# The first pair of heads loaded, cast and transposed head by head; batch 0's masks all on TensorE; PSUM banks from one list

## The chip, the cores and the metric

The kernel runs on one core of one Trainium2 chip. A core has TensorE (PE in the profile; PEld is its weight loads), VectorE (DVE), ScalarE (ACT), GpSimd (POOL) and SyncE (SP), which run side by side and wait for each other by semaphores. SP, ACT and POOL also issue the DMA transfers between DRAM and the on-chip memory SBUF. TensorE writes its results to PSUM, eight banks of 512 fp32 columns by 128 partitions. The metric is the device time of one execution in microseconds (us), lower is better.

## The reference

Attention over 4 batches, 8 heads, 768 positions and head size 64, followed by a two-layer feed-forward block with a PReLU. Heads 0, 2 and 6 ("retrieval") see all earlier positions; the other five ("streaming") see the first 4 positions and the last 64.

```
scores = scale * q @ k.T                      # per batch and head, 768 x 768
scores = where(mask, scores, -1e9)            # causal, or sink + window
a = softmax(scores);  x = a @ v               # 4 * 768 tokens of 8 * 64
h = x @ w_in                                  # 512 -> 2048
g = max(h, 0) + alpha * min(h, 0)
out = g @ w_out                               # 2048 -> 512
```

## The kernel before, in words

Heads are worked in pairs: pair n = 0 to 15, batch n // 4, heads PAIRS[n % 4] = (0,1), (2,3), (6,7), (4,5). Two heads of 64 fill the 128 partitions. A pair goes through these steps, and the document names them as the changed kernel does.

- Load: q, k and v by DMA into fp32 buffers (load_q L124, load_k L130, load_v L142), four buffers each. SP issues them, except pair 0's first k head and alpha, which ACT issues.
- Cast to bf16 (whole_q L179, whole_k L188, whole_v L208). In batch 0, pair 0's q is cast by VectorE for both heads at once (L183), its k by ScalarE for the first head and by VectorE for the second (L196); pairs 1 to 3 and all v of batch 0 are cast by GpSimd.
- Transpose: for pairs 0 to 7, six TensorE transposes each for q and k against an identity matrix (Tn, L291) into a PSUM bank, both heads at once. Tq (L298) is then copied to qT by ScalarE (L301), Tk (L303) to kT by VectorE (L314, L320 to L322), one head at a time; kT holds zeros in the other head's 64 partitions, so that a score matmul runs over 128 partitions. From pair 8 on, DMA transposes take their place.
- Scores S.n.head.part (S_retr L345, S_stream L378): matmuls of kT and qT into PSUM (L362, L393; L412 from pair 8), then the exponential by ScalarE into eR or eS (L370, L400, L415). In batch 0 a part uses two banks at once. The mask is either a further matmul of the identity with a tile of 0 and -30000, added into the same bank before the exponential (L365, L396), or a product with a 0/1 tile by VectorE after it (L375, L404, L420). In batch 0 TensorE adds all masks but those of pair 3's first head.
- A.n.head (AV, L452): 13 or 27 matmuls of eS or eR with v, whose column 64 of ones gives the softmax's sum; VectorE takes the reciprocal (L472) and multiplies (L473) into xn.
- X.n (L476): seven transposes of xn on TensorE and a copy to xT by VectorE (L487); for most pairs from 8 on, a DMA transpose.

A batch's 768 tokens then go through the feed-forward block as two token tiles, 512 and 256 wide, t = 0 to 7. P.t.f (P1, L505) is one bank of the first layer: four matmuls, one for each pair's 128 rows of xT (L516), ScalarE's ReLU of the negative (neg, L523) and VectorE's product and sum into g (L526). O.t.s.u (P2, L531) is a quarter of the second layer's 16 matmuls for 128 tokens (L536); after the fourth, ScalarE copies to ot (L541) and a DMA writes it out (L544).

The order of the work is that of the instructions as the Python code emits them; each engine runs its own in that order. First come the fills, the making of the masks, 36 matmuls of the identity with itself (L592 to L594) and pair 0's casts and transposes. A loop (L631) then lays out batch 0's pairs. Token tile 0's first blocks begin with the first three of their four matmuls (LEAD = 4 blocks, L657 to L667), with X3 between the second and the third block; then come the last columns and the other blocks. From pair 4 on, the attention of a batch is interleaved with the feed-forward work of the batch before by a budget (L712 to L731).

PSUM banks have fixed roles (L76): sc0 and sc1 for scores, m0 and m1 in turn for A, X and transposes, mm0, mm1, mm2 and m2 for the feed-forward block. ff_bank (L498) gives that block the bank which an assumed clock says is free first; before pair 4 and after pair 15 it may use the score banks too.

Of the kernel before, what the change touches and what calls it, by code (L numbers as in the profile page):

```python
# [10 lines left out]
DT = mybir.dt  # L11


@with_exitstack
def kernel(
# [60 lines left out]
    BANK = {"sc0": 0, "sc1": 1, "mm2": 2, "m2": 3, "mm0": 4, "mm1": 5, "m0": 6, "m1": 7}  # L76

    def bank(tag):
        return P[:, BANK[tag], :]

    def bank_bf(tag):
        return P[:, BANK[tag], :].bitcast(bf16)

# [80 lines left out]
    def load(n):  # L164
        load_q(n)
        load_k(n)
        load_v(n)

    natq, natk = {}, {}
# [7 lines left out]


    def whole_q(n):  # L179
        nat = natq[n] = NAT0[0][n] if n < 4 else NATQ[n % 2]  # L180
        copy = nc.gpsimd.tensor_copy if 0 < n < 6 else nc.scalar.copy if 0 < n < CROSS else nc.vector.tensor_copy
        flat = qf[n % NF].rearrange("p a b d -> p (a b d)")[:, 0:12 * D]
        copy(nat.rearrange("p i (h d) -> p h i d", h=2), flat.rearrange("p (h i d) -> p h i d", h=2, d=D))  # L183
        if n >= CROSS:
            nc.sync.dma_start(qT[n % NK][:, 0:S].rearrange("p (i r) -> p i r", r=128),
                              nat.rearrange("p i c -> p (i c)"), transpose=True)

    def whole_k(n):  # L188
        if n < CROSS:
            natk[n] = NAT0[1][n] if n < 4 else NATK1[n % 2]  # L190
            for hh, h in enumerate(heads(n)):
                copy = nc.gpsimd.tensor_copy if 0 < n < 6 else nc.scalar.copy if n == hh == 0 else nc.vector.tensor_copy

                T = row_tokens(n, h)
                flat = kf[n % NF].rearrange("p a b d -> p (a b d)")[:, 6 * D * hh:6 * D * (hh + 1)]
                copy(natk[n][:, :, D * hh:D * (hh + 1)].rearrange("p (t i) d -> p t i d", t=T),  # L196
                     flat.rearrange("p (i t d) -> p t i d", t=T, d=D))
            return
        flat = NATK[n % 2]
        rows = flat.rearrange("p (h x) -> p h x", h=2)[:, :, 0:896].rearrange("p h (t c) -> p h t c", c=128)  # L200
        nc.vector.tensor_copy(rows[:, :, :, 0:D], kf[n % NF].rearrange("p t h d -> p h t d"))
        sinks(n, rows)
        for hh, h in enumerate(heads(n)):
            nt = 6 if RETR[h] else 7
            nc.sync.dma_start(kTs[n % NK][hh][:, 0:128 * nt].rearrange("p (i r) -> p i r", r=128),
                              flat[:, 896 * hh:896 * hh + 128 * nt], transpose=True)

    def whole_v(n):  # L208
        vv = vb[n % NV]
        (nc.gpsimd if n < 6 else nc.vector).tensor_copy(vv[:, :, :, 0:D], vf[n % NF])  # L210
        sinks(n, vv.rearrange("p t h c -> p h t c"))

    for i in range(NF):
        nc.vector.memset(vf[i][:, 6, :, :], 0.0)
    load_q(0)
    load_k(0)
    alpha_r = wpool.tile([16, 128], fp32, name="alpha_r")
    nc.scalar.dma_start(alpha_r, moe_alpha.rearrange("(a p) -> a p", p=128))
    for n in range(1, 4):
        load_q(n)  # L220
        load_k(n)
        load_v(n - 1)
    load_v(3)

    zero = const.tile([128, 1], bf16, name="zero")
    nc.vector.memset(zero, 0.0)
    one = const.tile([128, 1], bf16, name="one")
    nc.vector.memset(one, 1.0)
    ident = const.tile([128, 128], bf16, name="ident")
    make_identity(nc, ident)  # L230
    ident_f = const.tile([16, 16], fp32, name="ident_f")
# [111 lines left out]
    def S_retr(n, hh, m):  # L343
        if m == 0:
            take_e(n, hh)  # L345
# [423 lines left out]
```

The softmax here doesn't subtract the row's maximum and nothing guards it: scores larger than these inputs give would overflow.

## Time and profile before

| | |
|---|---|
| median of 6 runs (range) | 242.29 us (241.66 to 242.57) |
| the profiled execution's own time | 242.38 us |
| its span, first to last instruction | 240.6 us |
| PE busy | 227.0 us (94%) |
| DVE busy | 165.3 us (69%) |
| ACT busy | 144.0 us (60%) |
| POOL busy | 43.8 us (18%) |
| granted TensorE clock, mean | 0.999 |

The page's busy times are of one profiled execution, on an axis that starts near its first instruction. A matmul's time includes its way through the array, so neighbouring matmuls overlap: "0.86 PE P L516 x4" in the chain is four matmuls one behind the other, 0.216 us each, though one alone shows 0.38 us. An engine's line with a bracket tells how long it stood idle before, and what came last of what it waited for. The chain of the page is followed back from the last instruction; it names the work that set the end. A few per cent of the matmul records can be missing.

By stages the profile falls into: fills and loads (0 to 5.7 us), batch 0's attention (5.7 to 28.4), the first feed-forward tile alone (28.4 to 43), attention of batches 1 to 3 with feed-forward work between (43 to 195), and the feed-forward rest (195 to 240.6).

### The profile page before, as it was taken

The page shows a single profiled execution, that of the slowest core. Times are in us where ns is not written, and L with a number is a line of the kernel's source. Part 1 is how long each engine was busy: PE and PEld are TensorE (multiplying, and loading weights), DVE is VectorE, ACT ScalarE, POOL GpSimd, SP SyncE. Part 2 cuts the span into 40 slices and gives each one's busy share as a digit, 9 for nine tenths or more (in the row PEclk, how much of TensorE's full clock was granted, in tenths as well). Part 3 has the DMA queues.
Part 4 walks back from the last instruction along what each step waited for, and adds up shares of the span by engine and source line. Part 5 has one row for each costly group of instructions (what it writes and reads, how often), then busy time and mean ns, then how long its engine had stood idle before and what let it go on. Part 6 is the DMA issues. An engine that isn't in the chain of part 4 may idle for free.

```text
span 240.6 us, 5234 instructions
## 1 busy us (share of the span) xinstructions
PE 227.0 (94%) x1987; PEld 143.5 (60%) x2017; DVE 165.3 (69%) x405; ACT 144.0 (60%) x265; POOL 43.8 (18%) x90
## 2 busy tenths in 40 slices
PE   6799899989987999999999999999999999999994
PEld 6688645557655755455666655556666544465553
DVE  7697878868798867989577858884665465633410
ACT  5888277847855757776655557866554354523220
POOL 5668960632010100000000000000000000000000
PEclk9999999999999999999999999999999999999999
DMA  6999999999999999999999992603131101011112
GB/s 207 294 239 171 226 204 197 246 279 248 253 213 131 245 191 226 211 167 216 199 224 203 225 175 66 120 3 77 46 78 44 46 0 45 0 61 73 44 44 90
DMA packets 90513, 36.25 MB, mean 151 GB/s; under 512 B 77672, under 2 KB 88696, under 8 KB 90488
## 3 DMA queue, kind: packets, MB, share of 16 engines
q1 hardware_dynamic: 84504, 26.66, 58.0%
q0 software_dynamic: 5664, 8.91, 16.5%
q10 hardware_dynamic: 320, 0.34, 0.5%
q8 instruction: 16, 0.26, 0.4%
q14 instruction: 9, 0.07, 0.1%
HBM read 27.55 MB, written 6.29 MB: 141 GB/s over the span
## 4 chain that ended last, share of the span: by engine, by line
PE 83%; DVE 7%; ACT 6%; issue 2%; ACTq 0%; DVEq 0%
PE P L516 34%; PE P L536 31%; PE P L467 6%; PE P L362 5%; ACT eR L370 2%; PE P L412 2%; PE P L291 2%; ACT eS L400 2%; PE P L553 1%; DVE xn L473 1%; PE P L486 1%; DVE g L526 1%; DVE eS L404 1%; PE P L393 1%; ACT neg L523 1%
## 5 line engine op out<-in xcount | busy, mean ns | idle before, releaser
L526 DVE SCALAR_TENSOR_TENSOR g<-neg,oma,P 128x512 bf16<-128x512 f32 (+1 forms) x128 | 74.7, 612 | 44.5 <-ACT neg L523 42.8
L516 PE MATMUL P<-xT,w_in_b 128*128 128x512 bf16 (+1 forms) x505 | 94.5, 325 | 0.4
L536 PE MATMUL P<-w_out_b,g 128*128 128x512 bf16 x345 | 88.7, 379 | 1.2
L523 ACT ACTIVATE neg<-P 128x512 f32<-128x512 f32 x96 | 57.2, 598 | 51.2 <-PE P L516 47.6
L516 PEld LDWEIGHTS <-w_in_b 128*128 128x128 bf16 x512 | 48.0, 98 | 29.3 <-issue 0.5
L536 PEld LDWEIGHTS <-g 128*128 128x128 bf16 x368 | 33.9, 98 | 30.1
L370 ACT ACTIVATE eR<-P 128x488 bf16<-128x488 f32 (+4 forms) x63 | 38.4, 620 | 13.7 <-PE P L362 11.8
L544 POOL DMA_DIRECT2D out_dram<-ot x18 | 9.8, 546 | 134.0 <-ACT ot L541 134.0
L362 PE MATMUL P<-qT,kT 128*128 128x488 bf16 (+17 forms) x132 | 24.7, 273 | 1.5 <-ACT eS L400 0.6
L473 DVE TENSOR_TENSOR xn<-P,rcp 128x448 bf16<-128x448 f32 x32 | 20.0, 624 | 1.1
L541 ACT COPY ot<-P 128x512 f32<-128x512 f32 x23 | 13.5, 587 | 9.0 <-PE P L536 8.6
L362 PEld LDWEIGHTS <-kT 128*128 128x128 bf16 x132 | 11.4, 97 | 9.9 <-issue 0.8
L415 ACT ACTIVATE eS<-P 128x352 bf16<-128x352 f32 x30 | 13.9, 462 | 5.7 <-PE P L412 5.7
L400 ACT ACTIVATE eS<-P 128x384 bf16<-128x384 f32 (+1 forms) x25 | 13.2, 558 | 4.6 <-PE P L393 4.0
L467 PE MATMUL P<-vb,eS 128*128 128x65 bf16 x260 | 11.9, 193 | 2.0 <-DVE eS L404 1.8
L467 PEld LDWEIGHTS <-eS 128*128 128x128 bf16 x260 | 10.6, 97 | 4.9 <-DVE eS L404 2.1
L467 PE MATMUL P<-vb,eR 128*128 128x65 bf16 x324 | 12.2, 192 | 1.1 <-DVE eR L375 1.1
L467 PEld LDWEIGHTS <-eR 128*128 128x128 bf16 x324 | 11.4, 97 | 2.9 <-DVE eR L375 1.2
L375 DVE TENSOR_TENSOR eR<-eR,mr_near 128x128 bf16<-128x128 bf16 (+5 forms) x36 | 8.2, 241 | 6.7 <-ACT eR L370 6.7
L420 DVE TENSOR_TENSOR eS<-eS,ms_near 128x352 bf16<-128x352 bf16 x30 | 10.1, 339 | 3.8 <-ACT eS L415 3.6
L393 PE MATMUL P<-qT,kT 128*128 128x192 bf16 (+2 forms) x70 | 10.0, 234 | 0.8 <-ACT eR L370 0.6
L412 PEld LDWEIGHTS <-kT 128*128 128x128 bf16 x70 | 6.6, 98 | 6.4
(97 smaller groups left out, 185.5 us busy)
## 6 DMA issues: line engine op xcount, KB each, us to landing
qf<-in_q_dram SPq DMA_DIRECT2D x16, 384.0 KB
out_dram<-ot POOLq DMA_DIRECT2D x18, 256.0 KB, 3.5
vf<-in_v_dram SPq DMA_DIRECT2D x22, 192.0 KB
kf<-in_k_dram SPq DMA_DIRECT2D x21, 192.0 KB
w_in_b<-in_moe_w_in_dram POOLq DMA_DIRECT2D x4, 512.0 KB, 8.5
w_out_b<-in_moe_w_out_dram POOLq DMA_DIRECT2D x4, 512.0 KB, 19.9
kf<-in_k_dram SPq DMA_DIRECT2D x9, 196.0 KB
vf<-in_v_dram SPq DMA_DIRECT2D x9, 196.0 KB
```

Source lines behind the costliest of these rows:

```text
L362: nc.tensor.matmul(sc[:, x, a - lo:z - lo], kt[:, 128 * j:128 * (j + 1)], qt[:, c:c + z - a], start=True, stop=not masked)
L370: nc.scalar.activation(e[:, lo:hi].rearrange("p (x c) -> p x c", x=len(parts)), sc[:, 0:len(parts), 0:(hi - lo) // len(parts)], AF.Exp, sc ...
L393: nc.tensor.matmul(sc[:, x, o:o + w], kt[:, 128 * j:128 * (j + 1)], qt[:, 124 * j:124 * j + w], start=True, stop=not on_pe)
L400: nc.scalar.activation(slots, sc[:, 0:len(thirds), 0:384].rearrange("p x (s c) -> p x s c", c=192), AF.Exp, scale=scale)
L415: nc.scalar.activation(slots, sc[:, 0:352].rearrange("p (s c) -> p s c", c=176), AF.Exp, scale=scale)
L467: nc.tensor.matmul(pav[:, i, :], e[:, o:o + 128], vv[:, j, hh, 0:D + 1], start=(m == 0), stop=(m == len(terms) - 1))
L473: nc.vector.tensor_tensor(xn[n][:, :, 64 * hh:64 * hh + 64], pav[:, :, 0:D], rcp.to_broadcast([128, NT, D]), op=ALU.mult)
L516: nc.tensor.matmul(psg[:, w * i:w * (i + 1)], w_in_b[:, a, 128 * fb:128 * (fb + 1)], xT[:, c, o:o + w], start=(c == 0), stop=(c == 3))
L523: nc.scalar.activation(neg, psg, AF.Relu, scale=-1.0)
L526: nc.vector.scalar_tensor_tensor(g_buf[t % 2][:, fb, 0:w], neg[:, c], oma[:, fb:fb + 1], psg[:, c], op0=ALU.mult, op1=ALU.add)
L536: nc.tensor.matmul(bank(po[t, s]), g_buf[t % 2][:, f, 128 * s:128 * (s + 1)], w_out_b[:, f, :], start=(f == 0), stop=(f == 15))
L541: nc.scalar.copy(ot, bank(po.pop((t, s))))
```

## The change

The kernel's steps become named items, each a function call, and a list ORDER says in which sequence they are emitted. A name is a step, its pair (or token tile) and its head or part: Lq0.0 is the load of q for pair 0's first head, C a cast, T transposes on TensorE and t their copy, S score matmuls, s the exponential, m a mask product, A and a, X and x, P, p (ReLU) and g (product and sum), O and o; kz, qz, vz, sz are fills.

Against the order before, the instructions of each engine differ in these places, all ahead of the eighth block of token tile 0; the rest of each engine's rows is the same and in the same order.

- Pair 0 is worked head by head. q is loaded by two DMAs, and k's second head is issued between them. VectorE casts q's first head, ScalarE k's first head; GpSimd casts the second heads of both. The first head's transposes take only its 64 columns. qT's other 64 partitions are filled with zeros at first (qz0, VectorE). The second head's k is transposed after S0.0.1 and its q after S0.0.2, directly ahead of pair 1's q; VectorE, not ScalarE, copies this q to qT.
- VectorE fills zero and one first; the fill of kT's second buffer (kz1) moves behind the cast of q's first head.
- 26 matmuls of the identity in place of 36.
- Pair 1's Tq stands after S0.0.2 (before: after S0.0.1), and Tk1 behind S0.1.0 (before: ahead of it).
- Pair 3's first head gets its mask from TensorE: seven matmuls (L396's kind) in place of two VectorE products (L404).
- In pair 3, S3.1.0 stands ahead of A2.1, and X2 ahead of A3.0.
- Token tile 0 begins five blocks with three of their four matmuls, and X3 stands after the third block.
- PSUM banks come from one list: take gives, of the banks allowed for a step, the one that was given back longest ago in the order of emission.

```diff
+ORDER = """
+id zero one vz0 vz1 vz2 vz3 Lq0.0 Lk0 Lq0.1 La Lq1 Lk1 Lv0 Lq2 Lk2 Lv1 Lq3 Lk3 Lv2 Lv3 nms nmr kz2 kz0 qz qz0 kz3 vo
+ro sz0 sz1 sz2 so idf Ck0.0 Cq0.0 kz1 Cq0.1 Ck0.1 warm Tq0.0 tq0.0 Tk0.0 tk0.0 Cq1 Ck1.0 Ck1.1 Cv0 Cq2 Ck2.0 Ck2.1 Cv1
+Cq3 Ck3.0 Ck3.1 wi0 Cv2 wi1 Cv3 gate wi2 wi3 wo0 wo1 wo2 wo3 Lq4 Lk4 Lv4 S0.0.0 s0.0.0 S0.0.1 s0.0.1 Tk0.1 tk0.1
+S0.0.2 s0.0.2 Tq0.1 tq0.1 Tq1 tq1 S0.1.0 s0.1.0 Tk1 tk1.0 tk1.1 S0.1.1 s0.1.1 Al al ms S1.0.0 s1.0.0 A0.0 a0.0 Tq2 tq2
+S1.0.1 s1.0.1 A0.1 a0.1 Tk2 tk2.0 tk2.1 S1.0.2 s1.0.2 S1.1.0 s1.1.0 X0 x0 S1.1.1 s1.1.1 S2.0.0 s2.0.0 A1.0 a1.0 Tq3
+tq3 S2.0.1 s2.0.1 A1.1 a1.1 Tk3 tk3.0 tk3.1 S2.0.2 s2.0.2 S2.1.0 s2.1.0 X1 x1 S2.1.1 s2.1.1 S3.0.0 s3.0.0 A2.0 a2.0
+S3.0.1 s3.0.1 S3.1.0 s3.1.0 A2.1 a2.1 S3.1.1 s3.1.1 X2 x2 A3.0 a3.0 nr ns Cq4 Ck4.0 Ck4.1 Cv4 kfz0 kfz1 kfz2 kfz3 nz0
+nz1 Lq5 Lk5 Lv5 Lq6 Lk6 Lv6 Lq7 Lk7 Lv7 A3.1 a3.1 P0.0.0 P0.0.1 P0.1.0 P0.1.1 P0.2.0 P0.2.1 X3 x3 P0.3.0 P0.3.1 P0.4.0
+P0.4.1 mr P0.0.2 p0.0 g0.0 P0.1.2 p0.1 g0.1 P0.5.0 P0.5.1 P0.5.2 p0.5 g0.5 P0.2.2 p0.2 g0.2 P0.6 p0.6 g0.6 P0.3.2 p0.3
+g0.3 P0.7 p0.7 g0.7 P0.4.2 p0.4 g0.4 P0.8 p0.8 g0.8 P0.9 p0.9 g0.9 P0.10 p0.10 g0.10 P0.11 p0.11 g0.11 P0.12 p0.12
...
-    BANK = {"sc0": 0, "sc1": 1, "mm2": 2, "m2": 3, "mm0": 4, "mm1": 5, "m0": 6, "m1": 7}
...
+    age = list(range(8))
+
+    def take(*choices):
+        got = min((c for c in choices if all(age[b] >= 0 for b in c)), key=lambda c: max(age[b] for b in c))
+        for b in got:
+            age[b] = -1
+        return got
+
+    def give(got):
+        for b in got:
+            age[b] = stamp[0]
+            stamp[0] += 1
+
...
-    def whole_q(n):
-        nat = natq[n] = NAT0[0][n] if n < 4 else NATQ[n % 2]
-        copy = nc.gpsimd.tensor_copy if 0 < n < 6 else nc.scalar.copy if 0 < n < CROSS else nc.vector.tensor_copy
-        flat = qf[n % NF].rearrange("p a b d -> p (a b d)")[:, 0:12 * D]
-        copy(nat.rearrange("p i (h d) -> p h i d", h=2), flat.rearrange("p (h i d) -> p h i d", h=2, d=D))
-        if n >= CROSS:
...
-    for i in range(NF):
-        nc.vector.memset(vf[i][:, 6, :, :], 0.0)
-    load_q(0)
-    load_k(0)
-    alpha_r = wpool.tile([16, 128], fp32, name="alpha_r")
-    nc.scalar.dma_start(alpha_r, moe_alpha.rearrange("(a p) -> a p", p=128))
-    for n in range(1, 4):
-        load_q(n)
-        load_k(n)
-        load_v(n - 1)
-    load_v(3)
-
...
-    nc.vector.memset(kT_all[:, 0].bitcast(fp32), 0.0)
-    nc.vector.memset(qT_all[:, :, S:S + 32].bitcast(fp32), 0.0)
-    nc.gpsimd.memset(kT_all[:, 3].bitcast(fp32), 0.0)
-    nc.vector.memset(kT_all[:, 1].bitcast(fp32), 0.0)
...
+    MISC = [(6,), (7,)]
+    SC = [(0,), (1,)]
+    SC2 = [(0, 1), (2, 3)]
+    FF = [(2,), (3,), (4,), (5,)]
+    LEAD = [(4,), (5,), (3,), (2,), (0,), (1,)]
+    TAIL = [(b,) for b in (2, 3, 4, 5, 0, 1, 6, 7)]
...
+    def cast_q0(hh):
+        natq[0] = NAT0[0][0]
+        cast_of("VP"[hh])(natq[0][:, :, D * hh:D * (hh + 1)], part_of(qf[0], hh).rearrange("p (i d) -> p i d", d=D))
...
+    def cast_k(n, hh):
+        nat = natk[n] = NAT0[1][n] if n < 4 else NATK1[n % 2]
+        T = row_tokens(n, heads(n)[hh])
+        cast_of("AP"[hh] if n == 0 else CK[n])(nat[:, :, D * hh:D * (hh + 1)].rearrange("p (t i) d -> p t i d", t=T),
+                                               part_of(kf[n % NF], hh).rearrange("p (i t d) -> p t i d", t=T, d=D))
...
+    def to_array(key, nat, choices, first_half=False):
+
+        held[key] = take(*choices)
+        tr = bank_bf(held[key][0])
         for i in range(6):
-            nc.tensor.transpose(tr[:, 128 * i:128 * (i + 1)], nat[:, i, :], ident)
+            if first_half:
+                nc.tensor.transpose(tr[0:D, 128 * i:128 * (i + 1)], nat[:, i, 0:D], ident)
+            else:
+                nc.tensor.transpose(tr[:, 128 * i:128 * (i + 1)], nat[:, i, :], ident)
+
+    def put_q(key, n, rows, copy):
+        tr = bank_bf(held[key][0])
+        cast_of(copy)(qT[n % NK][rows, 0:S].rearrange("d (p t) -> d p t", t=T), in_order(tr[rows, 0:S], T))
+        give(held.pop(key))
+    def put_k(key, n, hh, done=True):
+        h = heads(n)[hh]
+        T = row_tokens(n, h)
+        rows = slice(64 * hh, 64 * hh + 64)
+        kt = kTs[n % NK][hh][rows, :]
+        src = in_order(bank_bf(held[key][0])[rows, 0:S], T)
+        copy = cast_of("A" if n >= 4 and hh == 0 else "V")
+        if done:
+            give(held.pop(key))
...
-        on_pe = n < 3 or n == 3 and hh == 1
...
-                                 qt[:, 124 * j:124 * j + w], start=True, stop=not on_pe)
-                if on_pe:
+                                 qt[:, 124 * j:124 * j + w], start=True, stop=n >= 4)
+                if n < 4:
...
-        if not on_pe:
-            factor = (ms5 if thirds[0] == 2 else ms).unsqueeze(1).to_broadcast([128, len(thirds), 2, 192])
...
+        held["A", n, hh] = got = take(*MISC)
...
-    def ff_bank(where):
-        tag = min(BANKS[where], key=lambda x: free_at.get(x, 0.0))
-        free_at[tag] = float("inf")
-        return tag
...
+    def P1(t, f, cs, choices):
...
+        if cs[0] == 0:
+            held["P", t, f] = take(*choices)
...
-    warm = bank("m2")
-    for i in range(36):
-        nc.tensor.matmul(warm[:, 0:128], ident, ident, start=True, stop=True)
+        held["w"] = got = take((3,))
+        for i in range(26):
+            nc.tensor.matmul(bank(got[0])[:, 0:128], ident, ident, start=True, stop=True)
+        give(got)
...
-    LEAD = 4
-    for f in range(2):
-        P1(0, f, range(3), where="lead")
-    X(3)
-    for f in range(2, LEAD):
-        P1(0, f, range(3), where="lead")
-    nc.vector.tensor_scalar(mr, nmr, 0.0, None, op0=ALU.is_equal)
-    P1(0, 0, range(3, 4))
-    for f in range(1, LEAD):
-        P1(0, f, range(3, 4))
-        P1(0, f + LEAD - 1, where="lead")
-    for f in range(2 * LEAD - 1, 16):
...
+    for i in (0, 1):
+        fill(f"kz{i}", kT_all[:, i].bitcast(fp32), 0.0)
+    item("kz2", nc.scalar.copy, kT_all[:, 2].rearrange("p h c -> p (h c)"), zero.to_broadcast([128, 2 * 7 * 128]))
+    fill("qz0", qT_all[D:128, 0, 0:S].bitcast(fp32), 0.0)
...
+        item(f"Lq0.{i}", nc.sync.dma_start, part_of(qf[0], i), dram(q, i * S * D, [[6 * D, 128], [1, 6 * D]]))
+        item(f"Cq0.{i}", cast_q0, i)
+        item(f"Tq0.{i}", lambda i=i: to_array(("q0", i), natq[0], MISC, i == 0))
+        item(f"tq0.{i}", put_q, ("q0", i), 0, slice(D * i, D * i + D), "AV"[i])
+        item(f"Tk0.{i}", lambda i=i: to_array(("k0", i), natk[0], [(4,), (5,)], i == 0))
+        item(f"tk0.{i}", put_k, ("k0", i), 0, i)
...
+            if t == 0 and f < 6:
+                for part, cs in enumerate((range(0, 2), range(2, 3), range(3, 4))):
+                    item(f"P0.{f}.{part}", P1, 0, f, cs, LEAD)
...
+    for name in ORDER:
+        I[name]()
```

## The prediction

> **What bounds the kernel now.** I read the page's busy shares and its chain first, then the windows by stage (busy us of PE, PEld, DVE, ACT, POOL), then the timeline of the first 32 us.
>
> ```profile
> PE 227.0 (94%) x1987; PEld 143.5 (60%) x2017; DVE 165.3 (69%) x405; ACT 144.0 (60%) x265; POOL 43.8 (18%) x90
> ...
> PE 83%; DVE 7%; ACT 6%; issue 2%; ACTq 0%; DVEq 0%
> ```
>
> ```profile
> 28.40:46.00 17.60, 17.46 (x101) 8.99 (x102) 14.47 (x26) 12.41 (x22) 7.05 (x22) 1.00 1.20 216
> ```
>
> TensorE carries the run. From 28.4 to 46 us it is busy 17.46 of 17.60 us, so whatever moves the start of the first P1 block moves the end with it, unless a later stall gives way. Before 28.4 us it is not TensorE's work that counts but the hand-over between engines:
>
> ```profile
> 5.10 0.54 DVE L183 CAST g<-qf 128x768 bf16<-128x768 f32 x1
> 5.63 0.36 DVE L196 CAST g<-kf 128x384 bf16<-128x384 f32 x1
> 6.24 0.80 ACT L301 COPY qT<-P 128x768 bf16<-128x768 bf16 x1 [1.10 <-PE P L291]
> 6.67 1.01 DVE L314 COPY kT<-P 64x258 bf16<-64x258 bf16 x2 [0.68 <-PE P L291]
> 7.15 0.36 PE L362 MATMUL P<-qT,kT 128*128 128x454 bf16 x1 [0.51 <-DVE kT L314]
> 8.84 0.36 PE L362 MATMUL P<-qT,kT 128*128 128x106 bf16 x2 [0.23 <-ACT eR L370]
> 9.42 0.50 PE L291 MATMUL P<-ident,g 128*128 128x128 bf16 x6
> 9.95 0.95 DVE L314 COPY kT<-P 64x768 bf16<-64x768 bf16 x1 [1.10 <-PE P L291]
> 10.17 0.96 ACT L370 ACTIVATE eR<-P 128x910 bf16<-128x910 f32 x1
> 10.99 1.23 ACT L400 ACTIVATE eS<-P 128x768 bf16<-128x768 f32 x2
> 12.58 0.93 ACT L370 ACTIVATE eR<-P 128x908 bf16<-128x908 f32 x1 [0.36 <-PE P L365]
> ```
>
> A line gives start, busy time, engine, source line, operation, and in brackets the idle time before it with what ended it. The reader sees three things. The DVE cast of q at 5.10 is what the first transposes, copies and scores wait for in turn. S0.0.2, at 8.84, waits for the first exponential to free its bank, and Tk1 at 9.42 waits for nothing. VectorE, which makes every kT copy, has 1.10 us of slack before 9.95 and then none until 15.35 (its window 9.95 to 15.35 holds 5.20 busy of 5.40 us). Pair 3's end runs through VectorE's mask products, and the first P1 block's ReLU and product set when a bank comes free:
>
> ```profile
> 23.94 0.56 DVE L404 TENSOR_TENSOR eS<-eS,ms 128x768 bf16<-128x768 bf16 x1 [0.46 <-ACT eS L400]
> 25.19 0.97 DVE L404 TENSOR_TENSOR eS<-eS,ms 128x384 bf16<-128x384 bf16 x1
> 27.77 0.55 PE P L467 x13
> 31.55 1.68 ACT L523 ACTIVATE neg<-P 128x512 f32<-128x512 f32 x3 [5.23 <-PE P L516]
> 32.18 1.40 DVE L526 SCALAR_TENSOR_TENSOR g<-neg,oma,P 128x512 bf16<-128x512 f32 x2 [1.33 <-ACT neg L523]
> ```
>
> **The change part by part.** Times are of the profiled execution (242.38 us, span 240.6 us, so 1.78 us around it); the runs' median is 242.29. "Before" is read off the timeline, "after" is worked out.
>
> 1. First head's path. VectorE drops one zero fill of kT (0.81) from ahead of the cast, and gains a fill of 64x384. No row shows that shape: bounds 0.33 (the 128x328 fill) and 0.81 (128x896); I take 0.38, since the size is near the first. The cast starts at 5.10-0.81+0.38=4.67 and, now one head wide, lasts 0.36 (the 128x384 row): it ends at 5.03 instead of 5.64. Transposes follow 0.06 later, at 5.09. ACT's cast of k ends at 5.15 as before, so the six k transposes go behind the six of q (0.056 each, 0.34), at 5.43. ACT's qT copy starts 0.54 after the first transpose, as 6.24 did after 5.70: 5.63, plus 0.80, is 6.43. The kT copy starts at 5.96 and its first part ends at 6.39; the kz1 fill, 5.03 to 5.84, fits ahead of it. The first score matmul goes from 7.15 to 6.49: **-0.66** (-0.71 to -0.23 by the fill's bounds).
>
> 2. Second head's path, a new wait. S0.0.2 starts 1.69 after the first score (8.84-7.15), because it needs the bank that the first exponential frees: 8.18. Only then come the transposes of q's second head, 0.58 later as Tk1's did (9.42-8.84): 8.76. Their copy is VectorE's: it starts 0.53 later (9.95-9.42), at 9.29, and takes 0.95 by the kT row of the same shape, so S0.1.0 starts at 10.29 instead of 9.70. Behind S0.1.0 stands Tk1, which waited for nothing before: eight matmuls of 0.082 later, 10.95. Its copy tk1.0 runs 11.48 to 12.43 instead of from 9.95, and pair 1's first score starts at 12.47 instead of 11.88. From first score to first score that is 5.98 against 4.73: **+1.25**. A gain is excluded, since S1.0.0 reads this copy and the copy starts later; the ends are 0, if the exponentials' own pace covered it, and 1.25. I take 1.25: before, only 0.04 lay between the bank's release (11.84) and this score, so nothing covers it. ACT shows it as idle time of about 0.6 and 0.8 us before its first eS and before S1's exponential.
>
> 3. VectorE's backlog. From tk1.0's start to tk2.0's it worked 5.40 us without a pause, so tk2.0 runs 16.88 to 17.83 and S2.0.0 starts at 17.88 instead of 17.17: +0.71, **+0.12** beyond the +0.59. VectorE then regains its idle 0.63 before 18.67.
>
> 4. Masks of head 3.0. VectorE loses 0.56+0.97; TensorE gains seven matmuls, 0.082 each of 192 columns and less for the narrow ones, 0.50 in all. S3.0.0 goes from 22.51 to 23.22. Then on TensorE in order: 0.66 to 23.88, A2.0 0.81 to 24.69, S3.0.1 0.35 to 25.04, S3.1.0 0.66 to 25.70, A2.1. Its result is read 0.59 after its start, as A3.1's is (27.77, 28.36): 26.29; reciprocal and product end 0.86 later, 27.15; X2 starts at 27.20, VectorE's xT copy starts 0.63 later (27.00, 27.63) and takes 0.55: 27.83 to 28.38. A3.1 now takes the bank that X2 used, so it waits for this copy: 28.43, and P1 follows 0.39 later at 28.82. Before, A3.1 at 27.77 put P1 at 28.16 (its weights load at 28.12). So +0.66 there: the step brings **-0.05**. What is late next is TensorE's own longer queue and the bank. Ends: -1.53 if all of VectorE's time came back, +0.50 if only TensorE's work counted; I take the walk, which lies between.
>
> 5. Five P1 blocks instead of four ahead of their last column. From P0.0's last column to P0.6, which reuses its bank, there are now 7 matmuls of 0.216 (1.51); before there were 12 (2.59). The bank needs 0.42 (a matmul of 0.38 and the hand-over), 0.63 to the product (32.18-31.55), 0.70 for it and 0.05: 1.80. TensorE waits **+0.29** (0 to 0.29).
>
> 6. At nothing. Of TensorE's rows after P0 none moves; the banks there are renamed one to one (2, 3, 4, 5 to 5, 2, 4, 3; 6 and 7 swapped), so reuse distances stay. One more DMA issue on SP (0.47) puts every later load back by at most that; POOL waits for the first of them until 6.86 and its two new casts (0.51 each) lie ahead of that, while Tq1 is not due before 9.1. Uncovered it would cost 0.47. w_in's third and fourth pieces are issued at 23.2 and 23.9 and land at most 12.8 us later, 36.7; P0.12, four matmuls ahead of the transposes at 39.77, is due at 38.9 before and later now. If that cover were gone, TensorE would wait for the weights instead.
>
> Sum: -0.66+1.25+0.12-0.05+0.29=+0.95; 242.38+0.95=243.3, and the same on the median.
>
> **The clock.** Warm-up matmuls fall from 36 to 26.
>
> ```profile
> L594 PE MATMUL P<-ident x27: 287/314/314, 1.4 to 4.2; 128*128 128x128 bf16 x27
> ...
> L594 PE MATMUL P<-ident x11: 219/223/314, 4.1 to 4.9; 128*128 128x128 bf16 x11
> ```
>
> They start at 1.4, stand 0.107 apart and last 314 ns until about 4.6, then 219 ns. Twenty-six of them end near 4.2, ahead of that change, and TensorE then idles until 5.09. If it stays slow through the first scores, twelve transposes cost 12x0.051+0.095=0.7 more and the first 1164 score columns about 0.5: +1.2. I take 0, since most of the same stretch is still busy; both ends are kept.
> [...]
>
> **The rivals.**
> Cold start: as above, 243.3+1.2=244.5. For it speaks that the 26 end ahead of 4.6; against it that the gap to 5.09 is short.
> Absorbed: ScalarE's gaps of 0.36 (12.58), 0.22 (13.73) and 0.42 (17.92) shrink and swallow the 0.59 with which pair 1 begins and the 0.12 after it; what is left is -0.05+0.29, 242.6. Against it: all three gaps are waits for TensorE, and it waits there for the same late VectorE copies.
> Faster: the masks were the true end of pair 3, and all 1.53 us of VectorE come back in place of 0.05: 243.33-1.48=241.9. For it speaks that the chain runs through both L404 rows; against it that TensorE's own list fills 23.22 to 26.1 without a pause and that A3.1 has the bank to wait for. It decides from where A3.1 starts before 27.5 (28.43-0.95), the start at which nothing is lost.
>
> **How the numbers follow.** Forecast 0.45, with its own range 242.8 to 243.9 (the fill's bounds, the wait at P0.6, the SP issue); cold start 0.20; absorbed 0.17; faster 0.18. About 0.2% (0.48 us) is what a measurement can tell from no change: forecast and cold start are slower, 0.65; absorbed is within, 0.17; 0.18 faster. The range takes most of the rivals: 241.9 to 244.6.
>
> **What would show it.** Right: first score near 6.5; TensorE waiting for the DVE qT copy before S0.1.0 and for DVE kT near 12.5; tk2.0 ending near 17.8; A3.1 released by DVE xT near 28.4; a wait of 0.3 for DVE g before P0.6. Wrong: transposes at 5 us still lasting 314 ns; S1.0.0 released by ACT; P1 starting before 28.

## The result and the profile after

The changed kernel takes 243.92 us (median of 21 runs, 242.54 to 244.78), the kernel before 242.37 beside it (47 runs): 1.0061 of it, 95% interval 1.0048 to 1.0074, some 1.5 us slower. The profiled execution took 243.61 us (span 241.8) against 242.38 (240.6): +1.23, so the walk below follows a little less than the median shows. Each ratio below is to executions of the kernel before taken beside it; a median is over all executions, a ratio and its interval leave out those that were slow as a whole.

Busy times and chain of the page of the changed kernel, then a window of 17.6 us from its first feed-forward blocks (busy us of PE, PEld, DVE, ACT, POOL):

```profile
PE 228.6 (95%) x1996; PEld 144.6 (60%) x2026; DVE 163.8 (68%) x404; ACT 144.1 (60%) x265; POOL 44.8 (19%) x92
...
PE 84%; DVE 9%; ACT 4%; issue 2%; ACTq 0%; DVEq 0%
```

```profile
30.30:47.90 17.60, 17.28 (x98) 8.70 (x99) 14.43 (x25) 12.21 (x22) 7.60 (x19) 1.00 1.20 216
```

TensorE still carries the run, and still has next to no idle time once the feed-forward blocks have begun. VectorE is 1.5 us less busy, the two mask products that are gone, and that buys nothing at the end. The difference arises ahead of these blocks. The timeline of the changed kernel there:

```profile
4.79 0.34 DVE L309 CAST g<-qf 128x384 bf16<-128x384 f32 x1
5.19 1.49 PE L346 MATMUL P<-ident,g 128*64 128x128 bf16 x12 [0.80 <-DVE g L309]
6.08 0.79 ACT L353 COPY qT<-P 64x768 bf16<-64x768 bf16 x1 [0.95 <-PE P L346]
7.19 0.56 PE L405 MATMUL P<-qT,kT 128*128 128x454 bf16 x1 [0.51 <-DVE kT L368]
8.38 0.93 ACT L415 ACTIVATE eR<-P 128x908 bf16<-128x908 f32 x1 [1.51 <-PE P L408]
9.53 0.94 DVE L372 COPY kT<-P 64x744 bf16<-64x744 bf16 x1 [1.80 <-PE P L348]
11.60 0.26 PE L444 MATMUL P<-qT,kT 128*128 128x192 bf16 x1 [0.82 <-DVE qT L353]
12.80 0.95 DVE L368 COPY kT<-P 64x768 bf16<-64x768 bf16 x1 [1.26 <-PE P L348]
13.81 0.37 PE L405 MATMUL P<-qT,kT 128*128 128x454 bf16 x1 [0.54 <-DVE kT L368]
14.52 0.93 ACT L415 ACTIVATE eR<-P 128x908 bf16<-128x908 f32 x1 [0.86 <-PE P L408]
```

The cast of q's first head ends at 5.13 instead of 5.64 and the transposes start 0.51 earlier, yet the twelve take 1.49 us instead of 0.94 and the first score comes at 7.19, no earlier than before (7.15). Its exponential is 0.52 late, the first score of pair 1 at 13.81 is 1.93 late, and ahead of it stand two waits that the profile before did not have: TensorE waits 0.82 for VectorE's qT copy before S0.1.0, and 0.54 for the kT copy before S1.0.0.

Why the transposes are slow is seen in the answer for the identity tile (counts, duration in ns as min/median/max, first and last start):

```profile
L642 PE MATMUL P<-ident x26: 289/314/314, 1.4 to 4.1; 128*128 128x128 bf16 x26
...
L346 PE MATMUL P<-ident,g x12: 314/314/317, 5.2 to 6.4; 128*64 128x128 bf16 x12
```

The warm-ups (but for one of 289) last 314 ns and all twelve transposes 314 to 317, where the twelve of the kernel before took 216 to 229. A 128x128 matmul took 0.31 us as well where a later profile shows the clock granted at half (26 warm-ups in the kernel before, below). The record of the granted clock has the full rate from 8.96 us on; before, it had it from 4.60.

At the end of batch 0's attention:

```profile
28.44 0.56 PE L523 MATMUL P<-ident,xn 128*128 128x128 bf16 x7 [0.62 <-DVE xn L511]
29.04 0.56 DVE L528 COPY xT<-P 128x768 bf16<-128x768 bf16 x1 [0.66 <-PE P L523]
29.65 0.55 PE L501 MATMUL P<-vb,eS 128*128 128x65 bf16 x13 [0.26 <-DVE xT L528]
...
34.09 2.17 ACT L548 ACTIVATE neg<-P 128x512 f32<-128x512 f32 x4 [5.68 <-PE P L543]
35.52 1.24 PE L543 MATMUL P<-xT,w_in_b 128*128 128x512 bf16 x5 [0.17 <-DVE g L555]
```

A3.1 now waits for VectorE's xT copy, as the prediction had it, and starts at 29.65 against 27.77, +1.88; then P0.6 waits for the product that frees its bank. By the sixteenth ReLU of token tile 0 the lag is 2.22. Then something is given back: the first output copy is only 1.29 late, and from there to the end of VectorE's last copy all fourteen profiles of this study take the same 179.3 us. So all is decided in the first 60 us.

The table follows that for some of the profiles (us; the experiments are told below).

| | before | after | 36 warm-ups | four leading blocks | all four repairs | repairs, later w_out |
|---|---|---|---|---|---|---|
| full clock from | 4.60 | 8.96 | 4.82 | 4.07 | 5.95 | 4.52 |
| first score | 7.15 | 7.19 | 6.59 | 6.59 | 7.04 | 6.59 |
| pair 1's first exponential | 12.58 | 14.52 | 13.32 | 13.32 | 13.27 | 12.82 |
| pair 2's | 17.92 | 19.86 | 18.67 | 18.66 | 18.61 | 18.16 |
| pair 3's | 23.10 | 25.37 | 24.18 | 24.17 | 24.12 | 23.67 |
| 16th ReLU of tile 0 | 43.23 | 45.45 | 44.26 | 43.92 | 43.87 | 43.42 |
| first output copy | 58.57 | 59.86 | 58.56 | 58.97 | 59.36 | 58.24 |
| own time | 242.38 | 243.61 | 242.32 | 242.72 | 243.03 | 241.94 |

### The profile page after: what moved, and what is told of

It reads as the page before. It is cut to its first block, busy times and chain, and to the rows that moved or that the text cites. A ratio compares the mean times of both kernels' runs of the same rounds, so it can differ in the third digit from the quotient of the medians.

```text
span 241.8 us, 5256 instructions
## 1 busy us (share of the span) xinstructions
PE 228.6 (95%) x1996; PEld 144.6 (60%) x2026; DVE 163.8 (68%) x404; ACT 144.1 (60%) x265; POOL 44.8 (19%) x92
## 4 chain that ended last, share of the span: by engine, by line
PE 84%; DVE 9%; ACT 4%; issue 2%; ACTq 0%; DVEq 0%
PE P L543 32%; PE P L563 31%; PE P L501 7%; PE P L405 6%; PE P L438 2%; DVE g L555 2%; PE P L579 1%; PE P L523 1%; PE P L348 1%; PE P L444 1%; DVE kT L372 1%; ACT eR L415 1%; DVE eR L425 1%; ACT neg L548 1%; ACT eS L469 1%
## 5 line engine op out<-in xcount | busy, mean ns | idle before, releaser
L405 PE MATMUL P<-qT,kT 128*128 128x488 bf16 (+17 forms) x132 | 25.6, 280 | 1.8 <-DVE kT L368 1.1
L425 DVE TENSOR_TENSOR eR<-eR,mr_near 128x128 bf16<-128x128 bf16 (+5 forms) x36 | 8.2, 241 | 6.7 <-ACT eR L415 6.7
```

What stands on the lines that cost most here:

```text
L405: nc.tensor.matmul(sc[:, x, a - lo:z - lo], kt[:, 128 * j:128 * (j + 1)], qt[:, c:c + z - a], start=True, stop=not masked)
```

## The experiments

My theory after the result: the cold clock costs about 1.2 us, the late q copy of the second head and the order of Tk1 some 0.6, the five leading blocks 0.3. The rivals: that the order and not the clock is the larger part; that GpSimd's casts, meeting VectorE's products, set the end.

**One repair at a time, in the changed kernel.**

```diff
-        for i in range(26):
+        for i in range(36):
```


> The changed kernel with 36 warm-up matmuls again instead of 26. Cold-clock theory: the changed kernel's profile granted full clock only from 8.96 us, so its first transposes lasted 314 ns and its first score started at 7.19; with 36 the clock is full by about 4.6 to 5, the transposes last 219 ns, the first score starts near 6.5, pair 1's first score near 12.5 instead of 13.81, and the first P1 block 1.3 us earlier. At the end 0.9 to 1.3 us come back (ratio to before 1.000 to 1.002). Rival, that the order alone is to blame: the first score moves, but the second head's copies still set pair 1's start, and no more than 0.3 us comes back.

Measured: 242.74 us, 1.0026 of before (1.0006 to 1.0046), against 1.0061 (1.0048 to 1.0074) with 26. The intervals just do not meet. Of the timeline:

```profile
4.82 0.39 PE L642 MATMUL P<-ident 128*128 128x128 bf16 x4
5.19 0.86 PE L346 MATMUL P<-ident,g 128*64 128x128 bf16 x12
6.59 0.35 PE L405 MATMUL P<-qT,kT 128*128 128x454 bf16 x1 [0.55 <-ACT qT L353]
12.61 0.37 PE L405 MATMUL P<-qT,kT 128*128 128x454 bf16 x1 [0.54 <-DVE kT L368]
13.32 0.93 ACT L415 ACTIVATE eR<-P 128x908 bf16<-128x908 f32 x1 [0.86 <-PE P L408]
```

The transposes start at the same 5.19 but take 0.86 instead of 1.49. The first score comes 0.56 ahead of the kernel before, and pair 1's exponential 1.20 ahead of the changed kernel's. So ten more warm-ups, the last of which end just as the transposes become due, are worth 0.0035, some 0.85 us of the 1.5. The wait for VectorE's kT (0.54) is still there.

```diff
-S0.1.0 s0.1.0 Tk1 tk1.0 tk1.1 S0.1.1
+Tk1 tk1.0 tk1.1 S0.1.0 s0.1.0 S0.1.1
```


> The changed kernel with Tk1 and its copies moved ahead of S0.1.0 in the list, nothing else. Order theory: Tk1 no longer stands behind the wait for the q copy, its kT copy follows the q copy on VectorE at once (about 11.6 instead of 12.80), pair 1's first score starts near 12.6 instead of 13.81, the first P1 block 1.1 to 1.3 us earlier, and the end 0.8 to 1.2 us earlier (ratio to before 1.001 to 1.003). Rival, that only the cold clock is to blame: pair 1's first score moves by under 0.3 us, since the late first exponentials set it.

Measured: 243.11 us, 1.0033 (1.0014 to 1.0051). In its profile pair 1's first exponential comes only 0.13 earlier than in the changed kernel (14.39):

```profile
11.94 0.95 DVE L368 COPY kT<-P 64x768 bf16<-64x768 bf16 x1
11.96 0.26 PE L444 MATMUL P<-qT,kT 128*128 128x192 bf16 x1 [0.38 <-DVE qT L353]
12.83 1.19 ACT L469 ACTIVATE eS<-P 128x768 bf16<-128x768 f32 x2 [0.72 <-PE P L447]
13.70 0.35 PE L405 MATMUL P<-qT,kT 128*128 128x454 bf16 x1 [0.40 <-ACT eS L469]
```

VectorE's kT copy (tk1.0) is 0.86 earlier and no longer holds S1.0.0; the exponential eS, whose bank it needs, holds it in its place, 0.40. Besides, the slow clock lasted to 9.76 here, and the second head's transposes and copies stand 0.35 later for it. Without that delay about 0.5 would have been seen at S1.0.0. Two later profiles with Tk1 ahead, those of the last two columns of the table, bear this out: from the first score to S1.0.0 they take 5.54 us, against 6.02 with 36 warm-ups alone and 4.73 in the kernel before.

```diff
-P0.0.0 P0.0.1 P0.1.0 P0.1.1 P0.2.0 P0.2.1 X3 x3 P0.3.0 P0.3.1 P0.4.0 P0.4.1 mr P0.0.2 p0.0 g0.0 P0.1.2 p0.1 g0.1 P0.5.0
+P0.0.0 P0.0.1 P0.1.0 P0.1.1 X3 x3 P0.2.0 P0.2.1 P0.3.0 P0.3.1 mr P0.0.2 p0.0 g0.0 P0.1.2 p0.1 g0.1 P0.4.0 P0.4.1 P0.4.2
```


> The changed kernel with the P1 blocks of the first token tile in the order of the kernel before: four blocks ahead of their last column, X3 after the second. Theory (bank wait at P0.6): the first P1 block stays near 30.0, TensorE's wait for VectorE's product before P0.6 goes, the first tile is done 0.3 to 0.4 us earlier, and so is the end. Rival, that the wait is hidden: under 0.1 us.

Measured: 242.88 us, 1.0039 (1.0015 to 1.0062). This profile, with 26 warm-ups, happens to have the full clock from 4.07, so it stands beside the one with 36: equal to 0.01 us up to pair 3's exponential, and 0.34 ahead at the sixteenth ReLU (43.92 against 44.26). No wait for a product is left in the first blocks:

```profile
28.85 1.46 PE L543 MATMUL P<-xT,w_in_b 128*128 128x512 bf16 x6
30.14 0.55 PE L523 MATMUL P<-ident,xn 128*128 128x128 bf16 x7
30.53 8.80 PE L543 MATMUL P<-xT,w_in_b 128*128 128x512 bf16 x40
```

The 0.34 does not reach the end in this profile: the first output copy is 0.41 later than with 36 warm-ups (58.97 against 58.56), because at its new time a mask product of VectorE meets GpSimd's casts and A4.0 waits for it:

```profile
48.20 1.41 DVE L425 TENSOR_TENSOR eR<-eR,mr 128x136 bf16<-128x136 bf16 x3
49.39 0.72 PE L501 MATMUL P<-vb,eR 128*128 128x65 bf16 x18 [0.98 <-DVE eR L425]
```

The same 26 warm-ups end in a warm start here (full clock from 4.07 us) and in a cold one (from 8.58 to 9.76) in four other profiles, all five with the same instructions up to the first score: the start was a matter of the execution here.

```diff
-Cv4 kfz0 kfz1 kfz2 kfz3 nz0 nz1
+kfz0 kfz1 kfz2 kfz3 nz0 nz1 Cv4
```


> The changed kernel with GpSimd's six zero fills (kfz, nz) put ahead of the cast of v for pair 4, where it idles for 9.7 us. Theory (collision): a VectorE mask product on 128x132 that lasts 1.36 us at 47.5 while GpSimd casts pair 5's q and k (47.3 to 48.6) falls back to about 0.22 us, as the casts move to about 45 us; in the changed kernel nobody waits for that product, so the end moves by less than 0.3 us. Rival, that the long product has nothing to do with GpSimd: it stays over 1 us.

Measured: 243.86 us, 1.0054 (1.0029 to 1.0079), no different from the changed kernel. The product did not fall back to 0.22: GpSimd's cast of pair 5's q waited 1.04 for its load and stood at 47.84, and a product beside it took 0.90.

**All four together.**

> The changed kernel with all four edits: 36 warm-up matmuls, Tk1 ahead of S0.1.0, four leading P1 blocks, GpSimd's fills ahead of v's cast. If the causes are the ones named and lie one behind the other on the path, it gains 0.66 at the first score over the kernel before, keeps it to the first P1 block (about 27.5 against 28.16), loses nothing there, and has no collision at A4.0 (another 1.0): 240.6 to 241.2 us where the kernel before has 242.4 (ratio 0.993 to 0.996). Rival, that a later wait takes the gain: 242 or more.

Measured: 242.56 us, 1.0008 (0.9990 to 1.0026): the loss is gone within what can be told, but the gain that the expectation drew (240.6 to 241.2 us) did not come; its rival, a later wait, did. The four single gains (0.0035, 0.0028, 0.0022, 0.0007) add up to 0.0092, of which 0.0053 came. Of the single ones only that of the warm-ups is clear of the changed kernel's interval; the sizes of the others rest on the profiles.

**The same from the side of the kernel before.**

```diff
-    for i in range(36):
+    for i in range(26):
```


> The kernel before with 26 warm-up matmuls instead of 36, nothing else. Cold-clock theory: its transposes at 5.70 last 314 ns, its first score moves from 7.15 to about 7.8, pair 1's first score by 1.0 to 1.3 us, and the end by 0.5 to 1.2 us to the late side. Rival, that 26 are enough and the changed kernel's cold start has another reason (its own gap before the first transposes): no change within 0.2 us.

Measured: 243.35 us, 1.0025 (1.0001 to 1.0049). Its twelve times fall into two groups, six from 241.90 to 242.95 and six from 243.75 to 244.71. That these are warm and cold starts is not shown: the two executions with the lowest mean clock, 0.992 and 0.993, lie one in each group. Two windows of 3.4 us of its profile (the last three columns are granted clock, DMA share and GB/s):

```profile
4.00:7.40 3.40, 1.48 (x17) 0.92 (x16) 2.55 (x10) 1.93 (x3) 1.27 (x2) 1.00 1.10 346
7.50:10.90 3.40, 3.40 (x27) 2.65 (x26) 1.37 (x4) 2.61 (x4) 2.05 (x5) 0.50 1.19 294
```

The clock was full from 4.07, TensorE was then busy 1.48 of 3.40 us, and the next 3.41 us were granted at half (0.50 in the second window; mean of the execution 0.993). Among these profiles the first full grant comes from 4.07 to 9.76 us; what sets the moment of a grant or of its loss, no run shows.

The first score was on time here (7.20), unlike what the expectation drew; the clock went after it. Pair 1's first exponential is 0.89 late, the sixteenth ReLU only 0.27, since pair 3's second mask product takes 0.35 where it took 0.97 before (the row at 25.19 above, which ends with GpSimd's issue of a w_out load), and the first output copy is 0.91 late again, behind a cast of GpSimd:

```profile
26.09 0.35 DVE L404 TENSOR_TENSOR eS<-eS,ms 128x384 bf16<-128x384 bf16 x1
50.58 0.51 PE L291 MATMUL P<-ident,natq 128*128 128x128 bf16 x6 [1.00 <-POOL natq L183]
```

So a lag from the clock at the start and the lag at the end need not be the same microsecond.

```diff
+    for i in range(NF):
+        nc.gpsimd.memset(kf[i][:, 6, :, :], 0.0)
+    for nat in NATK:
+        nc.gpsimd.memset(nat.bitcast(fp32), 0.0)
     whole_v(4)
-    for i in range(NF):
-        nc.gpsimd.memset(kf[i][:, 6, :, :], 0.0)
-    for nat in NATK:
-        nc.gpsimd.memset(nat.bitcast(fp32), 0.0)
```


> The kernel before with GpSimd's six zero fills put ahead of the cast of v for pair 4. Collision theory: in its profile a VectorE mask product lasts 1.49 us near 47.6 while GpSimd casts pair 5's q and k (47.73 to 49.0), and A4.0 waits 1.1 us for it; with the casts gone to about 45.4 the product lasts 0.22 us, A4.0 does not wait, and the end is 0.7 to 1.1 us earlier (ratio 0.996 to 0.997). That would also say why the changed kernel, 2.3 us late after the first token tile, ends only 1.2 us late. Rival, that the changed kernel made up that microsecond by slack elsewhere: the end moves by under 0.3 us.

This looks for what the changed kernel got back after 45 us. In the kernel before, VectorE, GpSimd and TensorE show there:

```profile
47.45 1.78 DVE L375 TENSOR_TENSOR eR<-eR,mr 128x136 bf16<-128x136 bf16 x3
47.73 0.81 POOL L183 CAST natq<-qf 128x768 bf16<-128x768 f32 x1
48.50 0.50 POOL L196 CAST natm<-kf 128x384 bf16<-128x384 f32 x1
49.14 0.57 PE L467 MATMUL P<-vb,eR 128*128 128x65 bf16 x13 [1.08 <-DVE eR L375]
```

Three mask products take 1.78 us while GpSimd casts (the middle one 1.49, where such a product alone takes 0.22), and TensorE waits 1.08 for them at A4.0. In the changed kernel a long product, 1.36 of the 1.63, stands beside the same two casts, but it is of an earlier part, and A4.0 waits for nothing:

```profile
47.29 1.63 DVE L425 TENSOR_TENSOR eR<-eR,mr 128x128 bf16<-128x128 bf16 x3
47.30 0.81 POOL L305 CAST natq<-qf 128x768 bf16<-128x768 f32 x1
...
49.50 1.49 PE L501 MATMUL P<-vb,eR 128*128 128x65 bf16 x27
```

Measured with the fills moved: 241.98 us, 0.9982 (0.9962 to 1.0003), not to be told from before. In its profile the wait at A4.0 fell to 0.35, and the tile's sixteenth ReLU came 0.28 earlier, but the first output copy at 58.58 is where it was:

```profile
46.82 0.82 POOL L183 CAST natq<-qf 128x768 bf16<-128x768 f32 x1 [1.08 <-DMA qf<-in_q_dram]
52.23 0.51 PE L291 MATMUL P<-ident,natm 128*128 128x128 bf16 x6 [0.45 <-POOL natm L196]
54.42 0.83 ACT L183 CAST natq<-qf 128x768 bf16<-128x768 f32 x1 [0.86 <-DMA qf<-in_q_dram]
55.75 0.35 PE L362 MATMUL P<-qT,kT 128*128 128x455 bf16 x1 [0.31 <-ACT eR L370]
```

GpSimd's casts for pair 5 and ScalarE's for pair 6 now wait for their loads, and TensorE for a cast. The profile with all four repairs shows the same, ScalarE waiting 1.49 for pair 6's q, cast at 55.21.

**The masks.** In pair 3, head 0, VectorE multiplies again:

```diff
-                if n < 4:
+                if n < 3 or n == 3 and hh == 1:
                     nc.tensor.matmul(sc[:, x, o:o + w], ident, (nms6 if j == 6 else nms)[:, 0:w],
...
-                if n >= 4:
+                if n >= 4 or n == 3 and hh == 0:
                     item(f"m{n}.{hh}.{m}", M_retr if RETR[h] else M_stream, n, hh, m)
```


> The changed kernel with the mask of pair 3's first head multiplied by VectorE again, as before, instead of added by TensorE. By the prediction's step 4 (-0.05) the first P1 block and the end move by less than 0.3 us either way. Rival, that the masks set the end of pair 3: 1 to 1.5 us later.

Measured: 243.95 us, 1.0075 (1.0048 to 1.0103), not to be told from the changed kernel. The profiled execution lost the full clock once more, from 29.69 to 33.10 us (its mean was 0.993), and its second product took 1.39, so the rows of that stretch do not tell what the masks alone do; the same edit is tried again below.

**Is it the transfers?** In the last four kernels the third and fourth load of w_out are issued later, to leave more of the transfers to pairs 5 and 6. In the kernel before, with GpSimd's fills moved as above:

```diff
-    for i in range(4):
+    for i in range(2):
         load_w_out(i)
...
     whole_v(4)
+    load_w_out(2)
...
+            if i == 2 and n == 4:
+                pre.append(lambda: load_w_out(3))
```


> The kernel before, with GpSimd's six fills ahead of pair 4's value cast and with the third and fourth load of w_out issued later (after that cast, and after pair 5's key casts). Theory T (transfers): up to about 55 us the loads set a floor; ScalarE's cast of pair 6's queries begins at 54.05 to 55.3 in every profile, and what TensorE is ahead by 43 us is lost there. With half a megabyte of w_out out of the way that load lands one to two us sooner: ScalarE's wait of 0.9 for it and TensorE's waits of 1.0 in all between 43 and 61 us shrink to 0.4 or less, the first output copy goes from 58.6 to 57.6-58.0, and the time is 0.995 to 0.997 of before. Theory C (the stretched VectorE product was all that was lost there): no change against the run with the fills alone, 0.998. If w_out's fourth load comes too late, TensorE waits for it at about 57.5 us.

Measured: 243.60 us, 1.0042 (1.0019 to 1.0066), slower. ScalarE waits for pair 6's q no more and casts it at 53.11 instead of 54.42 (fills alone), so the half of theory T that speaks of this load holds. The gain does not come:

```profile
48.20 0.57 PE L467 MATMUL P<-vb,eR 128*128 128x65 bf16 x13 [0.76 <-DVE eR L375]
54.83 1.02 PE L536 MATMUL P<-w_out_b,g 128*128 128x512 bf16 x4 [2.44 <-DMA w_out_b<-in_moe_w_out_dram]
```

TensorE waits 2.44 us for a piece of w_out that came too late, the danger that the expectation named, and 0.76 us for long products, which are back beside GpSimd's casts and its issues of w_out. The sixteenth ReLU comes at 42.59, the earliest of all profiles, the first output copy only at 60.05.

The changed kernel with the four repairs and the same two loads later:

```diff
-wi0 Cv2 wi1 Cv3 gate wi2 wi3 wo0 wo1 wo2 wo3 Lq4
+wi0 Cv2 wi1 Cv3 gate wi2 wi3 wo0 wo1 Lq4
...
-kfz0 kfz1 kfz2 kfz3 nz0 nz1 Cv4 Lq5
+kfz0 kfz1 kfz2 kfz3 nz0 nz1 Cv4 wo2 Lq5
...
-O0.0.0 Ck5.0 Ck5.1 S4.0.2
+O0.0.0 Ck5.0 Ck5.1 wo3 S4.0.2
```


> The changed kernel with all four repairs (36 warm-ups, Tk1 ahead of S0.1.0, four leading blocks, fills ahead of Cv4) and the two later w_out loads. Theory T: ScalarE's wait of 1.5 for pair 6's queries goes, the first output copy moves from 59.4 to 58.4-58.7, and the time is 0.996 to 0.999 of before, against 1.0008 with the repairs alone. Theory C: 1.0008 as with the repairs alone, since no stretched product was left there.

Measured: 242.90 us, 1.0021 (0.9999 to 1.0043). The profiled execution is the fastest of all profiles, 241.94, with its first output copy at 58.24:

```profile
48.10 0.82 PE L501 MATMUL P<-vb,eR 128*128 128x65 bf16 x18 [0.19 <-DVE eR L425]
53.02 1.02 PE L563 MATMUL P<-w_out_b,g 128*128 128x512 bf16 x4 [0.49 <-DMA w_out_b<-in_moe_w_out_dram]
```

ScalarE's wait of 1.49 is gone and the output copy comes 1.12 earlier than with the repairs alone. Of that, 0.45 stands already at the sixteenth ReLU, where the earlier clock shows; the 0.67 after it goes the way of theory T. The median does not follow: it is no better than that of the repairs alone. A wait for w_out has come in here too, 0.49 in this profile, and one profile does not tell how long it is in the other executions.

The same with pair 0 loaded, cast and transposed as a whole:

```diff
-Lq0.0 Lk0 Lq0.1 La
+Lq0 Lk0 La
...
-so idf Ck0.0 Cq0.0 kz1 Cq0.1 Ck0.1 warm Tq0.0 tq0.0 Tk0.0 tk0.0 Cq1
+so idf kz1 Cq0 Ck0.0 Ck0.1 warm Tq0 tq0 Tk0 tk0.0 tk0.1 Cq1
...
-S0.0.0 s0.0.0 S0.0.1 s0.0.1 Tk0.1 tk0.1 S0.0.2 s0.0.2 Tq0.1 tq0.1 Tq1 tq1 Tk1
+S0.0.0 s0.0.0 S0.0.1 s0.0.1 Tq1 tq1 S0.0.2 s0.0.2 Tk1
```


> The same as the last one, but with pair 0 loaded, cast and transposed as a whole again (loads, casts and copies on the engines of the kernel before). What is left of the change is TensorE's mask sums for pair 3, the list of banks and the order written out. If head by head costs what the warm profiles show at pair 1's first exponential (13.3 against 12.6), this is 0.5 to 0.7 us faster than the last one and within 0.2 us of the kernel before with the same repairs; if the head-by-head start is worth its earlier first score (6.59 against 7.15), it is up to 0.5 us slower than the last one. If the masks on TensorE cost anything, it stays above the repaired kernel before by 0.3 us or more.

Measured: 243.39 us, 1.0033 (1.0014 to 1.0053), not faster than head by head. This run is spoiled in part by its own making: the kz1 fill stood right ahead of VectorE's cast of q, which began at 5.76 instead of 5.10, and the first score came at 7.72. From first score to pair 1's first exponential it took 5.42 (7.72 to 13.14), as before (5.43), against 6.23 head by head (6.59 to 12.82). It also met two waits for long products, 0.97 and 0.54. What the head-by-head start costs once repaired is therefore read from the profiles, +0.24 at pair 1's first exponential (12.82 against 12.58), and not from these times.

The repairs and later loads, with pair 3's first mask on VectorE (the masks' edit as above):

> The changed kernel with the four repairs and the later w_out loads, with the masks of pair 3's first head multiplied on by VectorE again. By the prediction's step on the masks (0.05 us gained by TensorE's sums, the first of tile 0's matmuls held by VectorE's output copies anyway) it is within 0.2 us of the same kernel with TensorE's sums. If VectorE is what holds pair 3's end, it is 0.4 to 0.8 us slower; if TensorE's four more mask sums (about 0.1 us each) are on the path, 0.3 to 0.5 us faster.

Measured: 243.15 us, 1.0020 (0.9996 to 1.0045), against 1.0021 with TensorE's sums. From pair 2's first exponential to A3.1 it takes 9.66 us with VectorE's products and 9.79 with TensorE's sums. In the order of the changed kernel the masks decide next to nothing, as long as the products are not stretched. This profile had the full clock only from 7.32, in spite of its 36 warm-ups, and its transposes were as slow as with 26:

```profile
5.38 1.49 PE L346 MATMUL P<-ident,g 128*64 128x128 bf16 x12
```

None of these kernels is faster than the kernel before by more than the measurement can tell; the nearest is the kernel before with GpSimd's fills moved.

## Why the prediction was right or wrong

Slower was right. The 243.92 us lie in the wide range and 0.02 above the forecast's own, 242.8 to 243.9, and the walk holds almost row by row for a warm start. That the sum came this near to the time was luck: two terms that it did not have nearly cancel. The profile with 36 warm-ups lets each step be read without the clock:

| step | predicted | with full clock | what the rows show |
|---|---|---|---|
| 1, first head | -0.66 | -0.56 | first score 6.59 against 7.15 |
| 2, second head's q | +1.25 | +1.29 | first score to S1.0.0 6.02 against 4.73 |
| 3, VectorE's backlog | +0.12 | +0.02 | pair 2's first exponential 0.75 late, S1.0.0 0.73 |
| 4, masks | -0.05 | -0.06 | A3.1 28.46 against 27.77, +0.69 |
| 5, five leading blocks | +0.29 | +0.34 | 16th ReLU 1.03 late |
| sum at 43 us | +0.95 | +1.03 | |
| not foreseen, 43 to 59 us | 0 | -1.04 | first output copy 58.56 against 58.57 |
| clock | 0 (rival +1.2) | +1.20 to +1.30 | after minus 36 warm-ups, at pair 1 and at the first output copy |

The clock is where the likeliest case failed: it took 0 for it, from bounds of 0 and 1.2, "since most of the same stretch is still busy". In the profile of after the twelve transposes were slow, as its list of what would show it wrong had them, and the price of the rival "cold start" was right: 1.20 at pair 1's first exponential. A chance of 0.20 was far too small for it: of the six profiles with 26 warm-ups four were slow at the first score, and a fifth lost the clock behind it. The rest of step 1 came out 0.10 short: the cast of q began at 4.79, not at the 4.67 of the sum.

Step 2 was right in mechanism and size. What it did not tell is what comes next when Tk1 is put back: the bank that eS holds, 0.40 in the profile of that run, so that the order alone returns about 0.5 of the 1.25 (6.02 against 5.54).

Step 3's +0.12 did not come. The reason by the rows, argued and not tried: ScalarE's copies and exponentials set the pace from pair 1 to pair 2, 5.34 to 5.35 us in all three profiles.

Step 4 came out as walked, with A3.1 released by the xT copy. But the size is right only against this profile of the kernel before, whose second product took 0.97. From pair 2's first exponential to A3.1 it takes 9.84 us there and 9.22 in two profiles of the same order in which that product took 0.35 (26 warm-ups; later w_out loads); with TensorE's sums it is 9.79 in every profile. Against those two, step 4 costs 0.57: the walk did not ask why the smaller product, 128x384, was the longer one. The rival "faster", that VectorE's 1.53 us were the true end of pair 3, falls: putting the products back moves the ratio by 0.0001 in one pair of runs and not measurably in the other.

Step 5 was right up to 43 us: taking the fifth leading block away returns 0.34 at the sixteenth ReLU, as with five the matmul that waits for P0.6's bank starts 0.55 behind the one ahead of it instead of 0.216 (33.77 and 34.32, 36 warm-ups). What it is worth at the end is not shown: the profile loses it again before the first output copy, and the 0.0022 of the times is within the intervals.

Step 6 costed the loads at nothing by following pair 1's and w_in's only. Past 43 us the sum of the steps was carried to the end, on the strength of a window that ends at 46 us; the "later stall" that its first part allowed for has no term. The rival "absorbed" had the right idea in the wrong place: nothing was swallowed by ScalarE's gaps before 18 us, but the whole warm lag of 1.03 was between 43 and 59 us. Two things are seen there. The kernel before loses 1.08 us to a stretched VectorE product, and the changed one, coming at another time, loses nothing. And where this wait is taken away in the kernel before, waits for the loads of pairs 5 and 6 and their casts are next, and it is where it was at the first output copy and 0.0018 faster, unclear, in the times. Over the ten profiles without later w_out loads the way from the sixteenth ReLU to the first output copy takes from 14.15 to 15.98 us. How much of the 1.0 is the one and how much the other in an average execution stays open; the run of the kernel before that should have lifted the floor of the loads brought a wait for w_out instead.

The two unforeseen terms are +1.2 and -1.0, which is why a sum of +0.95 stands close to the +1.23 of the profile and the +1.5 of the times.

## What to carry to other kernels

A short warm-up that ends ahead of the first real work (TensorE idled 0.80 us between them in the changed kernel, 1.40 in the kernel before with 26) was here a gamble on the clock: two of the six profiles had it in full from 4.07 us, four only from 8.58 to 9.76. Count such a start as cold, and fill the gap with warm-ups until the work is due; here ten more were worth 0.0035. Even that was no promise: of the four profiles of the head-by-head start with 36 warm-ups, two had the full clock ahead of the first transposes (from 4.52 and 4.82 us), one during them (5.95) and one after them (7.32). Moving one operation behind another on the way to a new head start moved everything queued behind it on its engine (from the first score to S1.0.0 6.02 us in place of 4.73): read off the next holder (here a bank, 0.40) before pricing the repair. And the lag carried out of one stage was worth only what the next stage's transfers and collisions let through (1.03 us at 43 us, nothing at the first output copy, with 36 warm-ups), so read the waits of the stage after as well.

## What the runs showed of the hardware that was not expected

- With the same 26 warm-ups the full clock was granted from 4.07 us in two profiles and only from 8.58 to 9.76 in four; with 36 it came from 4.52 to 5.95, and once at 7.32. It was lost again for 3.41 us, from 7.48 in one profile and from 29.69 in another (mean of each execution 0.993); in the first TensorE had been busy 1.48 us of the 3.40 from 4.00 on.
- VectorE's products of two bf16 SBUF tiles (L375, L425, 128x128 to 128x144) between 43 and 60 us, over all fourteen profiles: they take 0.21 to 0.26 us, also while GpSimd fills a buffer; but 24 of them, begun beside a GpSimd cast or copy, take 0.31 to 1.49 and end 0.07 to 0.10 us after it (one, begun 0.01 us after a copy, took 0.22). Four more, 0.48 to 1.16, stand beside GpSimd's issue of a w_out load and end within 0.12 of its end; five beside its issue of an output copy took 0.22 to 0.23. Pair 3's product of 128x384 took 0.97 and 0.64 beside w_out issues in two profiles and 0.35 beside them in two others. Why a product is stretched beside a cast, a copy or an issue, and not beside a fill, no run shows.
